# Decay table rows by scaled exponentials, and the last down operand split ahead of the last up sums

## The chip, the cores and the metric

The kernel runs on one core of a Trainium2 chip. Its engines are named as in the profile: PE (matrix products; PEld is its weight load), DVE, ACT, POOL, and SP, which here only issues transfers. The metric is the device time of one execution in microseconds (us), the median of several runs.

## The reference

One block of a network: a state-space convolution and a bilinear gated unit, each behind a layer norm that is scaled and shifted by a conditioning vector. L is 2048, D is 640, N is 192, F is 1536.

```python
mod = (silu(c) @ w_mod).reshape(1, 6, 1, 640)          # sa, ca, ga, sb, cb, gb
h = layernorm(x) * (1 + ca) + sa                       # x is (1, 2048, 640)
# the convolution: one kernel K of length L for each channel d
A = dt * (A_re + 1j * A_im)                            # dt = exp(log_dt), A is (640, 192)
K = einsum("dn,dnl,dn->dl", C, exp(A[:, :, None] * arange(L)), dt * B).real
y = irfft(rfft(pad(K)) * rfft(pad(h.T)))[:, :L].T + h * Dskip
x = x + ga * y
h = layernorm(x) * (1 + cb) + sb
x = x + gb * (((h @ w_gate) * (h @ w_up)) @ w_down)
```

The change lies in exp(A l), whose absolute value is exp(dt A_re l), a decay, and in the last product, with w_down.

## The kernel before

**Tables.** The 640 channels are five blocks `db` of 128, and each block has two halves `hf` of four pieces, so there are 40 pieces `n`. A power exp(A l) is built from a decay and a phase. The positions l are split into high and low parts, so a decay table is an outer product of two short tables: `RH` (eleven rows of 96 numbers a half, for factors 1536, 1024, 512, 0, 8, 16 ... 56 of the logarithm of the decay) and `LP` (positions 64 l) or `LQ` (positions 0 to 7, grown by doubling from the rows of `RL`, whose factors are 1, 2, 4, with amplitudes in its fourth row).

`u_seeds(db)` is a generator that makes these seeds in segments named by letters. Those that matter: `s_d` shifts phases; `s_r(h)` multiplies the logarithms of the decay, which PE has transposed into PSUM (`ps`), by a small constant tile `mults` on DVE, into RL and RH (L521, L523); `s_x` takes a square root and an absolute value; `s_e` takes the exponentials on ACT (seven into LP with the constant scales 64 l, one over all of RH, one over RL, both in place); `s_f` works out the arctangent's argument; `s_g` copies the amplitudes into RL (L571) and takes the arctangent of `pta`; `s_h` transposes it on PE; `s_v` turns it into phases on DVE (L580), from which POOL makes its phase seeds (L584, L585). All of ACT's operations go through one helper and have the line L135. For the first block the halves go apart, the second half's exponentials late; from the second block on a segment does both halves together.

POOL then makes, piece by piece, the phases `Pha`, `Phb` and the decay products `EQ` (from LQ and RH) and `EP` (from LP and RH), all on L649. ACT takes sines and cosines of the phases (`tra`, `trb`), DVE multiplies these with EP and EQ (`k_mul`, L731: `QtA`, `PtAa`, `PtAb`, `QtB`, `PtB`), and PE sums them into the kernel (`kg`, L745 and L760). EP and EQ have two buffers, so POOL's piece n+2 waits until DVE has done the products of piece n. Between these stand the stages of the Fourier transforms (L782 to L942).

**The gated unit.** F is cut in twelve tiles `f`, and the tokens into two halves of two blocks `tb` each. Up and gate products are made with operands that are split into a high and a low part (`hilo`, L992: ACT writes the high part, DVE the difference). For a tile, `y_1`, `z_1`, `y_2`, `z_2`, `y_3` run matmuls (L1028) and sums of them on DVE (L1385, L1397, L1398, L1416, L1405) with the product on DVE (L1410) or POOL. `d_prep(tb, f)` splits a tile of activations and its down weights for the down products (`down`, L1455), and issues a transfer of further weights for odd f; its first two pairs go into `e` and `wsgh`, `wsgl`, the later ones into `sh`, `sl`.

**What sets the order.** Every engine's instructions stand in the order in which the program is written. In the table phase a table of numbers, `SCHED`, gives each step its slot; in the gated unit the order of the calls in the loop does. An engine that waits holds up all that stands behind.

Of the kernel before, what the change touches and what calls it, by code (L numbers as in the profile page):

```python
# [19 lines left out]
P = 128  # L20
D = 640
# [4 lines left out]
NF = F // P  # L26
# [12 lines left out]
    fo=(22003, 31003, 31005, 35001),  # L39
    e0=(-87000,),  # L40
    mc=((31004, 39005, 40006, 43001, 52000), (34000, 53002, 60000, 62000, 69002), (58000, 91004, 92001)),
    q=((22004, 32000, 39001, 40005, 42006, 44000, 44001, 44002, 51000, 51001, 56001, 56002, 57000, 57002), (66002, 89000, 95003, 101000, 107000, 107001, 111000, 112000, 123000, 123003, 124001, 131000, 131003, 131004), (137001, 175000, 176001, 186009, 188001, 189001, 197003, 197004, 201000, 201001, 203002, 204001, 204002, 206001), (210002, 226000, 252005, 264003, 265002, 268001, 268002, 268003, 268005, 272001, 275000, 277000, 280002, 281001)),
    pre=(((56000, 73001, 78000), (40007, 61001, 66003), (76004, 82000, 86001), (88001, 95001, 97002)), ((119002, 127004, 132000), (131002, 131005, 135002), (86005, 99001, 100000), (118000, 118003, 118005)), ((143001, 160000, 160003), (153002, 172001, 172003), (181000, 186005, 186007), (173000, 178000, 178001)), ((221001, 252001, 252006), (224002, 242001, 242004), (245001, 261000, 261001), (281002, 281005, 285000)), ((317000, 335000, 336003), (265003, 298000, 298001), (297000, 315001, 315002), (182002, 196000, 196001))),
    c=(((161005, 162006, 165000, 166001), (122000, 122002, 154000, 155002), (144001, 144002, 167002, 168004), (125000, 125002, 141001, 141002)), ((208003, 217002, 220007, 224000), (201002, 201003, 205000, 211000), (181001, 181002, 198000, 200001), (168003, 170002, 184001, 186003)), ((292002, 295005, 308002, 308006), (245002, 249000, 253002, 253003), (254006, 256002, 278002, 281004), (291000, 291006, 302001, 303000)), ((319002, 321001, 329000, 332001), (337001, 337008, 346000, 349002), (351000, 351001, 360000, 364002), (363002, 365005, 365009, 370000)), ((375000, 379000, 391000, 392004, 393000, 403000), (386001, 386002, 392000, 393001, 394000, 404000), (380002, 385001, 388005, 392001, 392002, 392003), (365006, 371002, 392005, 396000, 398000, 404001))),
    d=(((376000, 388003, 388004), (206000, 206003, 210000), (222000, 225000, 225001), (283001, 284003, 291002)), ((236000, 244002, 248001), (251001, 261002, 262001), (267001, 270000, 270002), (224004, 240000, 244001)), ((340000, 358000, 358001), (354000, 367000, 367002), (319004, 338000, 339005), (309002, 325001, 332000)), ((397001, 401001, 409000), (406000, 414001, 414002), (402000, 414000, 431011), (411000, 424000, 431009)), ((404002, 406001, 407000, 412002), (409002, 412001, 419000, 419001), (425001, 425002, 429000, 431003), (404003, 409001, 415000, 415001))),
# [27 lines left out]
    xs='ababaaaabababa',  # L73
)
SEG0 = ("l", "a", "b", "c", "ud", "r", "x", "e", "f", "G", "g", "D", "h", "v", "R", "")
SEG = ("l", "a", "b", "c", "ud", "D", "r", "R", "x", "E", "f", "g", "h", "v")
P_PH, P_EP, P_MOD = 3, 6, 1


# [50 lines left out]
def tile_kernel(ctx: ExitStack, tc: tile.TileContext, I, out):  # L130
# [3 lines left out]
    def act(o, i, f=AF.Copy, **kw):  # L134
        return S.activation(o, i, f, **kw)  # L135
# [13 lines left out]
    sm = const.tile([P, 16], F32, name="sm")  # L149
    halfpi, dt, dt2 = sm[:, 10:11], sm[:, 0:NB], sm[:, NB : 2 * NB]  # L150
    V.memset(halfpi, math.pi / 2)
    mults = const.tile([P, 14], F32, name="mults")
    for k, m in enumerate((1536, 1024, 512, 0, 8, 16, 24, 32, 40, 48, 56, 1, 2, 4)):
        V.memset(mults[:, k : k + 1], float(m))
    shl = const.tile([P, 11], I32, name="shl")
    for k in range(11):
        V.memset(shl[:, k : k + 1], k + 1)
# [259 lines left out]
    LQ = pk1.tile([P, 96, 8], F32, name="LQ")  # L417
    LP = pk1.tile([P, 3, 96, 8], F32, name="LP")
    LH = pk1.tile([P, 192, 8], I32, name="LH")
    V.memset(LP[:, :, :, 0], 1.0)  # L420
    RH = pk1.tile([P, 3, 11, 96], F32, name="RH")
    RL = pk1.tile([P, 2, 4, 96], F32, name="RL")
    DH = [pk1.tile([P, 4, 192], I32, name=f"DH{i}") for i in range(3)]
    DL = [pk1.tile([P, 4, 192], I32, name=f"DL{i}") for i in range(2)]
# [3 lines left out]
    def u_seeds(db):  # L428
# [10 lines left out]
        dc = dt[:, db : db + 1]  # L439
        hs = (slice(0, 4), slice(4, 8))  # L440
        Dh, Dl = ([R[(2 * db + h) % len(R)] for h in range(2)] for R in (DH, DL))
        Rh, Rl = ([R[:, (2 * db + h) % R.shape[1]] for h in range(2)] for R in (RH, RL))

        def halves(R, hh):

            a, b = ((2 * db + h) % R.shape[1] for h in (hh[0], hh[-1]))
            return R[:, a : a + len(hh)] if a <= b else R[:, 2::-2]
# [3 lines left out]
        T = {}  # L451
# [10 lines left out]
        def free(h, *kinds):  # L462

            hf = 2 * db + h
            for k_ in kinds:
                if k_ in ("ph", "ep", "eq") and hf >= 3:
                    need(1, k_, 4 * (hf - 3) + 3)
                elif k_ in ("lh", "lq") and hf >= 2:
                    need(1, k_, hf - 2)
# [46 lines left out]
            mark("step", 2 * db + h)  # L516

        def s_r(h):
            ps = T["ps"]
            free(h, "ep", "eq", "lq")  # L520
            V.tensor_tensor(g4(Rl[h])[:, 0:3], ps[:, 0, hs[h]].unsqueeze(1).to_broadcast([P, 3, 4, 24]),  # L521
                            mults[:, 11:14].unsqueeze(2).unsqueeze(3).to_broadcast([P, 3, 4, 24]), op=OP.mult)
            V.tensor_tensor(g4(Rh[h]), ps[:, 0, hs[h]].unsqueeze(1).to_broadcast([P, 11, 4, 24]),  # L523
                            mults[:, 0:11].unsqueeze(2).unsqueeze(3).to_broadcast([P, 11, 4, 24]), op=OP.mult)

        def s_u():
            V.tensor_tensor(u, u, T["q"][:, 0], op=OP.add)
# [5 lines left out]
            V.tensor_scalar(pe[:, 1], x, 0.0, 0.5, op0=OP.is_ge, op1=OP.subtract)  # L533

        def s_e(*hh):
            lp, rh, rl = (halves(R, hh) for R in (LP, RH, RL))
            for l in range(1, 8):
                act(lp[:, :, :, l], rl[:, :, 0], AF.Exp, scale=64.0 * l)
            act(rh, rh, AF.Exp)
            act(rl[:, :, 0:3], rl[:, :, 0:3], AF.Exp)  # L540
            for h in hh:
                mark("lp", 2 * db + h)

# [34 lines left out]
        def s_v():  # L578
# [8 lines left out]
            for h in range(2):  # L587
# [1 line left out]
            mark("seeds", db)  # L589

        one = lambda f, *a: lambda: f(*a)
        steps = dict(l=s_l, a=s_a, b=s_b, c=s_c, d=one(s_d, 0), D=one(s_d, 1), r=one(s_r, 0), R=one(s_r, 1), u=s_u, x=s_x,
                     e=one(s_e, 0), E=one(s_e, 0, 1), f=s_f, G=s_G, g=s_g, h=s_h, v=s_v)
        if db == 0:
            LATE.append(lambda: s_e(1))
# [816 lines left out]
    def y_3(i):  # L1412
        ps = pa(side=i % NF == NF - 1)
        prod(ps, [(WT[i], 6 + k, HX[1], k) for k in range(2)] + [(WU[i], 3, HX[1], 2)])
        c = S67.pop(i)
        V.tensor_tensor(c, ps, c, op=OP.add)  # L1416
        G.tensor_tensor(a_tile(NF + i % NF), c, ZT.pop(i), op=OP.mult)
# [107 lines left out]
    for half in range(2):  # L1525
        i0 = half * NF
        if half == 0:

            new_s()
            new_h2()  # L1530
            H = iter(T0["hd"])
            seq = [(sums_u, 0), (x_1, 2), (x_2, 2, False), (x_c, 2), (split_u, 0, "a"), (split_u, 0, "b")]
            seq += [(tokens2, 1, 1, 0, False), (tokens2, 1, 1, 2, True), (s_sums, 0), (tokens2, 1, 1, 1, False), (tokens2, 1, 1, 3, False), (s_sums, 1)]
            seq += [(tokens2, 1, 1, 4, False), (x_1, 3), (x_2, 3, False)]
            seq += [(s_split, k, j) for j in (2, 1) for k in range(2)] + [(s_one, 4), (split_u, 0, "c"), (s_split, 0, 3), (s_split, 1, 3)]
            seq += [(s_one, 2), (s_one, 3), (s_split, 0, 4), (s_split, 1, 4), (s_five,), (x_c, 3), (sums_u, 1), (raw,), (raw_u, 2), (res_l, 0, 1)]
            seq += [(y_1, 0), (split_g, AHEAD), (z_1, 0), (y_2, 0), (split_u, 1), (sums_u, 2), (raw_u, 3), (y_3, 0), (z_2, 0), (fold, 0)]
            for g_, *a_ in seq:
                at((next(H),), once(g_), *a_)
            due(433)  # L1540
            assert not jobs
            PRE[0] = False
        else:
            for j in range(AHEAD):
                if LEAD <= j + 1 < AHEAD:
                    split_g(i0 + j + 1)
                x_1(i0 + j)
                x_2(i0 + j)
# [12 lines left out]
            res_l(3, 1)
        for f in range(1 - half, NF):
            i = i0 + f
            y_1(i)
            if f + AHEAD < NF:
                split_g(i + AHEAD)
            z_1(i)
            late = 0 < f <= NF - AHEAD
            if late:
                x_1(i + AHEAD - 1)  # L1570
            y_2(i)
            if f + 1 < NF:
                split_u(i + 1)
            if f + 2 < NF:
                sums_u(i + 2)
            if f + 3 < NF:
                raw_u(i + 3)
            if late:
                x_2(i + AHEAD - 1)
            y_3(i)  # L1580
            z_2(i)
            if half == 0:
                fold(f)
            if f >= NF - 2:
# [38 lines left out]
```

## Time and profile before

| | |
|---|---|
| median of three runs | 964.85 us (964.2 to 965.12) |
| profiled execution | 960.78 us, of which the span of the trace 959.0 |
| granted PE clock, mean | 0.978 |
| busy PE, DVE, ACT, POOL | 863.3, 757.6, 569.7, 566.6 us |
| HBM traffic | 108.36 MB read, 38.86 MB written |

The span is one execution, from its first to its last record. A row of the timeline has the start, the time from there to the end of the last of its instructions, engine, line, operation, destination and sources, shape and count; a bracket at its end tells how long the engine stood idle before it and which instruction ended that. Rows overlap a little, since an engine starts the next instruction before the last has drained. The tables end near 420 us, the gated unit's products run from about 503 to 951.

### The profile page before, as it was taken

The page shows a single profiled execution, that of the slowest core. Times are in us where ns is not written, and L with a number is a line of the kernel's source. Part 1 is how long each engine was busy: PE and PEld are TensorE (multiplying, and loading weights), DVE is VectorE, ACT ScalarE, POOL GpSimd, SP SyncE. Part 2 cuts the span into 40 slices and gives each one's busy share as a digit, 9 for nine tenths or more (in the row PEclk, how much of TensorE's full clock was granted, in tenths as well). Part 3 has the DMA queues.
Part 4 walks back from the last instruction along what each step waited for, and adds up shares of the span by engine and source line. Part 5 has one row for each costly group of instructions (what it writes and reads, how often), then busy time and mean ns, then how long its engine had stood idle before and what let it go on. Part 6 is the DMA issues. An engine that isn't in the chain of part 4 may idle for free.

```text
span 959.0 us, 26424 instructions
## 1 busy us (share of the span) xinstructions
PE 863.3 (90%) x11070; PEld 715.4 (75%) x11070; DVE 757.6 (79%) x1328; ACT 569.7 (59%) x1022; POOL 566.6 (59%) x419
## 2 busy tenths in 40 slices
PE   2878876898798689889889999999999999999998
PEld 1565655676675467678568888889998888889998
DVE  8998688888889988888899777786677877687452
ACT  6899988887987879754773322225555322223330
POOL 5999999799799999940135866721021544451000
PEclk9977999999999899999999999999999999999999
DMA  8487575434455655478854355155536222212241
GB/s 304 150 289 243 164 222 194 138 112 129 139 183 157 178 148 159 126 228 245 234 157 121 99 192 180 40 192 165 193 137 219 84 83 82 83 55 84 82 166 55
DMA packets 141320, 148.94 MB, mean 155 GB/s; under 512 B 8208, under 2 KB 119568, under 8 KB 139792
## 3 DMA queue, kind: packets, MB, share of 16 engines
q1 hardware_dynamic: 139904, 145.80, 48.4%
q8 instruction: 87, 1.43, 0.6%
q10 hardware_dynamic: 1296, 1.44, 0.5%
q14 instruction: 33, 0.27, 0.1%
HBM read 108.36 MB, written 38.86 MB: 154 GB/s over the span
## 4 chain that ended last, share of the span: by engine, by line
PE 46%; DVE 6%; issue 1%; ACT 1%; POOL 1%; DMA 0%; SPq 0%; DVEq 0%; ACTq 0%
PE pa L1028 26%; PE pa L1455 17%; PE psg L1028 1%; DVE sl L992 1%; DVE wtl L992 0%; PE psg L1108 0%; DMA TVb<-WD 0%; PE psg L1455 0%; DVE a L1147 0%; DVE wsgl L992 0%; ACT hfb L135 0%; PE psg L1162 0%; DVE st L1081 0%; DVE xb L1468 0%; DVE hl L1149 0%
## 5 line engine op out<-in xcount | busy, mean ns | idle before, releaser
L649 POOL TENSOR_TENSOR EQ<-LQ,RH 128x1536 f32<-128x1536 f32 x40 | 124.1, 3103 | 1.1 <-DVE QtB L731 1.1
L135 ACT ACTIVATE z<-pa 128x512 f32<-128x512 f32 x24 | 14.3, 598 | 167.6 <-PE pa L1028 114.7
L992 DVE TENSOR_TENSOR wsgl<-wga,wsgh 128x640 fp32r<-128x640 f32 x72 | 67.6, 943 | 46.5 <-ACT wsgh L135 46.5
L135 ACT ACTIVATE wsgh<-wga 128x640 fp32r<-128x640 f32 x72 | 52.3, 732 | 66.5 <-PE pa L1455 30.2
L1399 POOL TENSOR_TENSOR z<-z,s 128x512 f32<-128x512 f32 x24 | 33.4, 1390 | 88.6 <-DVE s L1398 88.6
L1004 POOL TENSOR_TENSOR tf<-wur,wgb 128x256 f32<-128x256 f32 x24 | 18.8, 782 | 99.6 <-DVE wtl L992 58.9
L649 POOL TENSOR_TENSOR EP<-LP,RH 128x768 f32<-128x768 f32 x40 | 65.7, 1650 | 11.6 <-DVE PtB L731 11.5
L1455 PE MATMUL pa<-wsgh,sh 128*128 128x384 f32 (+1 forms) x295 | 68.6, 311 | 0.0
L1455 PE MATMUL pa<-wsgl,sh 128*128 128x384 f32 (+1 forms) x295 | 68.2, 310 | 0.0
L1455 PE MATMUL pa<-wsgh,sl 128*128 128x384 f32 (+1 forms) x295 | 68.2, 310 | 0.0
L649 POOL TENSOR_TENSOR Pha<-LH,DH 128x1536 int32<-128x1536 int32 (+1 forms) x21 | 62.4, 2971 | 1.3 <-ACT tra L135 1.1
L649 POOL TENSOR_TENSOR Phb<-LH,DH 128x1536 int32<-128x1536 int32 x20 | 62.2, 3112 | 0.0
L992 DVE TENSOR_TENSOR wtl<-tf,wth 128x256 fp32r<-128x256 f32 (+1 forms) x72 | 58.8, 843 | 0.0
L731 DVE TENSOR_TENSOR QtA<-tra,EQ 128x1024 f32<-128x1024 f32 x44 | 51.8, 1214 | 8.0 <-POOL LQ L643 3.2
L1397 DVE TENSOR_TENSOR s<-pa,s 128x512 f32<-128x512 f32 x24 | 16.6, 690 | 42.9 <-PE pa L1028 37.9
L731 DVE TENSOR_TENSOR QtA<-trb,EQ 128x1024 f32<-128x1024 f32 x36 | 42.7, 1215 | 9.6 <-ACT trb L135 3.9
L760 PE MATMUL kg<-QtB,PtB 64*32 64x64 f32 x2560 | 45.3, 220 | 4.3 <-issue 2.2
L760 PEld LDWEIGHTS kg<-QtB,PtB 64*32 64x32 f32 x2560 | 38.4, 108 | 11.8 <-issue 5.9
L1028 PE MATMUL pa<-sh,wtl 128*128 128x512 f32 x144 | 44.6, 391 | 0.9 <-DVE wtl L992 0.9
L1455 PEld LDWEIGHTS pa<-wsgh,sl 128*128 128x128 f32 x295 | 45.3, 188 | 0.0
L1455 PEld LDWEIGHTS pa<-wsgh,sh 128*128 128x128 f32 x295 | 45.3, 188 | 0.0
L1455 PEld LDWEIGHTS pa<-wsgl,sh 128*128 128x128 f32 x295 | 45.3, 188 | 0.0
(653 smaller groups left out, 2854.5 us busy)
## 6 DMA issues: line engine op xcount, KB each, us to landing
wga<-wdg SPq DMA_DIRECT2D x24, 640.0 KB, 4.3
wga<-B_w_gate SPq DMA_DIRECT2D x12, 640.0 KB, 5.9
wgb<-B_w_gate SPq DMA_DIRECT2D x24, 320.0 KB, 3.3
wur<-B_w_up SPq DMA_DIRECT2D x24, 320.0 KB, 4.0
xb<-x2d SPq DMA_DIRECT2D x6, 1280.0 KB, 8.6
t_ti<-w_mod SPq DMA_DIRECT2D x3, 1600.0 KB, 8.6
t_tw<-w_mod SPq DMA_DIRECT2D x3, 1600.0 KB, 9.5
WD<-Wa SPq DMA_DIRECT2D x8, 512.0 KB, 3.7
```

What stands on the lines that cost most here:

```text
L135: return S.activation(o, i, f, **kw)
L649: G.tensor_tensor(o.rearrange("p x (h l) -> p x h l", l=8), lo.unsqueeze(2).to_broadcast([P, rows, nh, 8]), hi.rearrange("p h x -> p x h") ...
L731: V.tensor_tensor(t, tr, e.unsqueeze(1).to_broadcast([P, 2, R, 32]), op=OP.mult)
L760: PE.matmul(kg[j * 32 : j * 32 + 32, dd, :], PtB[lo : lo + 64, c, r, :], QtB[lo : lo + 64, c, r, :], start=False, stop=dd == 7 and c == 1, ...
L992: V.tensor_tensor(lo, v, hi, op=OP.subtract)
L1004: G.tensor_tensor(t[:, 0:2], u[:, 0:2], g[:, 0:2], op=OP.subtract)
L1028: PE.matmul(ps, w[a][:, k], x[b][:, l], start=n == 0 and m == 0, stop=n == 2 and m == len(ks) - 1)
L1397: V.tensor_tensor(S67[i], ps, S6[i], op=OP.add)
L1399: G.tensor_tensor(ZT[i], ZT[i], S67[i], op=OP.add)
L1455: PE.matmul(ACC[tb][t][c], x[:, ts], w[:, cs], start=st, stop=f == NF - 1 and n == 2 and (one or t % 2 == 1))
```

## The change

`mults` and its fourteen memsets go; RH's row for factor 0 is set to 1.0 once. DVE no longer makes products: it copies the logarithms into RL's first row, one copy for both halves (for the first block one each). ACT makes each row of RH and RL with an exponential of its own, which reads that row and has the factor as its constant scale. RL's first row is written last, in place, and waits for the reads ahead of it on the same engine. Waits for free buffers of EP and EQ move from `s_r` to `s_e`. For each block from the second on, two segments become one, and a slot of the table `q` is dropped. In the gated unit `d_prep` of the last tile is called ahead of that tile's `y_3` and `z_2`.

```diff
-    q=((22004, ..., 44000, 44001, 44002, 51000, ...), ...
+    q=((22004, ..., 44000, 44001, 51000, ...), ...
-SEG = ("l", "a", "b", "c", "ud", "D", "r", "R", "x", "E", "f", "g", "h", "v")
+SEG = ("l", "a", "b", "c", "ud", "D", "S", "x", "E", "f", "g", "h", "v")
-    mults = const.tile([P, 14], F32, name="mults")
-    for k, m in enumerate((1536, 1024, 512, 0, 8, 16, 24, 32, 40, 48, 56, 1, 2, 4)):
-        V.memset(mults[:, k : k + 1], float(m))
+    V.memset(RH[:, :, 3], 1.0)
...
         def s_r(h):
-            ps = T["ps"]
-            free(h, "ep", "eq", "lq")
-            V.tensor_tensor(g4(Rl[h])[:, 0:3], ps[:, 0, hs[h]].unsqueeze(1).to_broadcast([P, 3, 4, 24]),
-                            mults[:, 11:14].unsqueeze(2).unsqueeze(3).to_broadcast([P, 3, 4, 24]), op=OP.mult)
-            V.tensor_tensor(g4(Rh[h]), ps[:, 0, hs[h]].unsqueeze(1).to_broadcast([P, 11, 4, 24]),
-                            mults[:, 0:11].unsqueeze(2).unsqueeze(3).to_broadcast([P, 11, 4, 24]), op=OP.mult)
+            for i in h:
+                free(i, "lq")
+            rl = RL[:, 0:2, 0].rearrange("p h (s r) -> p h s r", r=24)[:, h[0] : h[-1] + 1]
+            V.tensor_copy(rl, T["ps"][:, 0, hs[h[0]].start : hs[h[-1]].stop].rearrange("p (h s) r -> p h s r", s=4))
...
         def s_e(*hh):
+            for h in hh:
+                free(h, "ep", "eq")
             lp, rh, rl = (halves(R, hh) for R in (LP, RH, RL))
             for l in range(1, 8):
                 act(lp[:, :, :, l], rl[:, :, 0], AF.Exp, scale=64.0 * l)
-            act(rh, rh, AF.Exp)
-            act(rl[:, :, 0:3], rl[:, :, 0:3], AF.Exp)
+            for k in (2, 1, 0):
+                act(rh[:, :, k], rl[:, :, 0], AF.Exp, scale=512.0 * (3 - k))
+            for k in range(4, 11):
+                act(rh[:, :, k], rl[:, :, 0], AF.Exp, scale=8.0 * (k - 3))
+            for k in (2, 1, 0):
+                act(rl[:, :, k], rl[:, :, 0], AF.Exp, scale=float(2**k))
...
+            if f == NF - 1:
+                d_prep(2 * half, 1)
             y_3(i)
             z_2(i)
             if half == 0:
                 fold(f)
-            if f >= NF - 2:
-                d_prep(2 * half, f - NF + 2)
+            if f == NF - 2:
+                d_prep(2 * half, 0)
```

Line numbers move by two at most. The order on three engines' pieces follows, of before and of after. First DVE at the seeds of block 3 (near 248 us): `psfa` is PSUM, `psfc` the argument for the next step, L868 a Fourier stage.

```order
L731 TENSOR_TENSOR QtA<-tra,EQ_141 128x32x32 x2
L731 TENSOR_TENSOR PtAa<-trb,EP_143 128x1024
L521 TENSOR_TENSOR RL<-psfa,mults 128x288
L523 TENSOR_TENSOR RH<-psfa,mults 128x1056
L521 TENSOR_TENSOR RL<-psfa,mults 128x288
L523 TENSOR_TENSOR RH<-psfa,mults 128x1056
L731 TENSOR_TENSOR PtB<-tra,EP_143 128x512
L731 TENSOR_TENSOR QtB<-tra,EQ_141 128x16x32 x2
L533 TENSOR_SCALAR psfc<-ptb 128x192
```

```order
L733 TENSOR_TENSOR QtA<-tra,EQ_126 128x32x32 x2
L733 TENSOR_TENSOR PtAa<-trb,EP_128 128x1024
L520 COPY RL<-psfa 128x2x96
L733 TENSOR_TENSOR PtB<-tra,EP_128 128x512
L733 TENSOR_TENSOR QtB<-tra,EQ_126 128x16x32 x2
L529 TENSOR_SCALAR psfc<-ptb 128x192
```

Four products stand as one copy now, straight ahead of the same PtB. Second, ACT at the same block (near 255 us), from the table load for the square root to the arctangent of `pta`.

```order
L135 ACT_TABLE_LOAD
L135 ACTIVATE ptb<-ptb 128x192
L135 ACTIVATE psfc<-ptb 128x192
L135 ACT_TABLE_LOAD
L135 ACTIVATE LP<-RL 128x192 x7
L135 ACTIVATE RH<-RH 128x2112
L135 ACTIVATE RL<-RL 128x2x288
L135 ACT_TABLE_LOAD
L135 ACTIVATE trb<-PtAb 128x512
L135 ACTIVATE pta<-pta 128x192
```

```order
L135 ACT_TABLE_LOAD
L135 ACTIVATE ptb<-ptb 128x192
L135 ACTIVATE psfc<-ptb 128x192
L135 ACT_TABLE_LOAD
L135 ACTIVATE LP<-RL 128x192 x7
L135 ACTIVATE RH<-RL 128x2x96 x10
L135 ACTIVATE RL<-RL 128x2x96 x3
L135 ACT_TABLE_LOAD
L135 ACTIVATE trb<-PtAb 128x512
L135 ACTIVATE pta<-pta 128x192
```

Two long instructions are thirteen short ones; nothing else moved on ACT. Third, DVE at the end of the first token half's up products (near 634 us): `psg` is PSUM, `a` an activation tile, `e` and `wsgl` what the down products read.

```order
L1398 TENSOR_TENSOR s_8714<-z,s_8714 128x512
L1416 TENSOR_TENSOR s_8735<-psg,s_8735 128x512
L1405 TENSOR_TENSOR s_8714<-psg,s_8714 128x512
L1410 TENSOR_TENSOR a_8520<-a_8520,s_8714 128x512
L992 TENSOR_TENSOR e<-a_7456,e 128x512
L992 TENSOR_TENSOR wsgl<-wga,wsgh 128x640
L992 TENSOR_TENSOR sl<-a_7457,sh 128x512
```

```order
L1400 TENSOR_TENSOR s_8752<-z,s_8752 128x512
L994 TENSOR_TENSOR e<-a_7494,e 128x512
L994 TENSOR_TENSOR wsgl<-wga,wsgh 128x640
L1418 TENSOR_TENSOR s_8773<-psg,s_8773 128x512
L1407 TENSOR_TENSOR s_8752<-psg,s_8752 128x512
L1412 TENSOR_TENSOR a_8558<-a_8558,s_8752 128x512
L994 TENSOR_TENSOR sl<-a_7495,sh 128x512
```

The two split rows stand three rows earlier, behind the sums that are ready and ahead of those that wait for `psg`. The order on PE and POOL is as before.

More of the change, by code (lines that the diff above doesn't have):

```diff
@@ L41 @@
     mc=((31004, 39005, 40006, 43001, 52000), (34000, 53002, 60000, 62000, 69002), (58000, 91004, 92001)),
-    q=((22004, 32000, 39001, 40005, 42006, 44000, 44001, 44002, 51000, 51001, 56001, 56002, 57000, 57002), (66002, 89000, 95003, 101000, 107000, 107001, 111000, 112000, 123000, 123003, 124001, 131000, 131003, 131004), (137001, 175000, 176001, 186009, 188001, 189001, 197003, 197004, 201000, 201001, 203002, 204001, 204002, 206001), (210002, 226000, 252005, 264003, 265002, 268001, 268002, 268003, 268005, 272001, 275000, 277000, 280002, 281001)),
+    q=((22004, 32000, 39001, 40005, 42006, 44000, 44001, 51000, 51001, 56001, 56002, 57000, 57002), (66002, 89000, 95003, 101000, 107000, 107001, 111000, 123000, 123003, 124001, 131000, 131003, 131004), (137001, 175000, 176001, 186009, 188001, 189001, 197003, 201000, 201001, 203002, 204001, 204002, 206001), (210002, 226000, 252005, 264003, 265002, 268001, 268002, 268005, 272001, 275000, 277000, 280002, 281001)),
     pre=(((56000, 73001, 78000), (40007, 61001, 66003), (76004, 82000, 86001), (88001, 95001, 97002)), ((119002, 127004, 132000), (131002, 131005, 135002), (86005, 99001, 100000), (118000, 118003, 118005)), ((143001, 160000, 160003), (153002, 172001, 172003), (181000, 186005, 186007), (173000, 178000, 178001)), ((221001, 252001, 252006), (224002, 242001, 242004), (245001, 261000, 261001), (281002, 281005, 285000)), ((317000, 335000, 336003), (265003, 298000, 298001), (297000, 315001, 315002), (182002, 196000, 196001))),
@@ L419, in tile_kernel @@
     LH = pk1.tile([P, 192, 8], I32, name="LH")
+    RH = pk1.tile([P, 3, 11, 96], F32, name="RH")
     V.memset(LP[:, :, :, 0], 1.0)
-    RH = pk1.tile([P, 3, 11, 96], F32, name="RH")
+    V.memset(RH[:, :, 3], 1.0)
     RL = pk1.tile([P, 2, 4, 96], F32, name="RL")
@@ L441, in u_seeds @@
         Dh, Dl = ([R[(2 * db + h) % len(R)] for h in range(2)] for R in (DH, DL))
-        Rh, Rl = ([R[:, (2 * db + h) % R.shape[1]] for h in range(2)] for R in (RH, RL))
+        Rl = [RL[:, h] for h in range(2)]
         def halves(R, hh):
@@ L591, in u_seeds @@
         one = lambda f, *a: lambda: f(*a)
-        steps = dict(l=s_l, a=s_a, b=s_b, c=s_c, d=one(s_d, 0), D=one(s_d, 1), r=one(s_r, 0), R=one(s_r, 1), u=s_u, x=s_x,
+        steps = dict(l=s_l, a=s_a, b=s_b, c=s_c, d=one(s_d, 0), D=one(s_d, 1), r=one(s_r, (0,)), R=one(s_r, (1,)), S=one(s_r, (0, 1)), u=s_u, x=s_x,
                      e=one(s_e, 0), E=one(s_e, 0, 1), f=s_f, G=s_G, g=s_g, h=s_h, v=s_v)
```

## The prediction

> **What bounds the kernel now.** I read the page first, then busy time by stretches of 40 us, then the waits of the engine that is full in a stretch, then the rows around the edits. From the page, busy shares and the chain that ended last by line:
>
> ```profile
> PE 863.3 (90%) x11070; PEld 715.4 (75%) x11070; DVE 757.6 (79%) x1328; ACT 569.7 (59%) x1022; POOL 566.6 (59%) x419
> PE pa L1028 26%; PE pa L1455 17%; PE psg L1028 1%; DVE sl L992 1%; DVE wtl L992 0%; PE psg L1108 0%; DMA TVb<-WD 0%; PE psg L1455 0%; DVE a L1147 0%; DVE wsgl L992 0%; ACT hfb L135 0%; PE psg L1162 0%; DVE st L1081 0%; DVE xb L1468 0%; DVE hl L1149 0%
> ```
>
> These averages hide two halves. Stretches, with the busy us of PE, PEld, DVE, ACT and POOL:
>
> ```profile
> 80.00:120.00 40.00, 33.02 (x680) 23.51 (x682) 28.96 (x46) 38.51 (x66) 38.46 (x28) 0.87 0.66 210
> 520.00:560.00 40.00, 40.00 (x179) 33.11 (x178) 32.47 (x47) 10.59 (x24) 29.77 (x27) 1.00 0.49 153
> 600.00:640.00 40.00, 38.92 (x185) 32.54 (x184) 33.38 (x47) 11.42 (x25) 23.82 (x20) 1.00 0.30 104
> ```
>
> While tables are made (here 80 to 120) POOL is full and ACT as full; DVE has a quarter free. In the gated unit PE is full, but for 1.08 us in the last stretch. POOL's waits from 40 to 430 us, the longest three kinds that the edits can reach:
>
> ```profile
> POOL EP L649 <- DVE PtB L731: 11.5, 3, 6.3
> POOL EQ L649 <- DVE QtB L731: 1.1, 1, 1.1
> POOL DL L585 <- DVE ptb L580: 0.6, 1, 0.6
> ```
>
> So only about 13 us of table time are POOL's to lose by waiting, and what DVE saves counts only in them.
>
> **Part 1: products leave DVE.** DVE first, then ACT and POOL, around the seeds of block 3:
>
> ```profile
> 248.54 0.44 DVE L521 TENSOR_TENSOR RL<-psfa,mults 128x288 f32<-128x288 f32 x1
> 251.60 0.68 DVE L731 TENSOR_TENSOR PtB<-tra,EP 128x512 f32<-128x512 f32 x1
> 249.38 0.60 ACT L135 ACTIVATE tra<-ab 128x512 f32<-128x512 f32 x1
> 252.42 1.66 POOL L649 TENSOR_TENSOR EP<-LP,RH 128x768 f32<-128x768 f32 x1 [6.27 <-DVE PtB L731]
> ```
>
> The four products take 251.60-248.54 = 3.06 us a block, 1.53 a half; five blocks make 15.3. A copy of 128x2x96 takes their place, about 0.3 (the L580 row below moves as many elements in 0.36), five make 1.5. DVE loses 13.8 us, nearly all beside POOL's work. Only in block 3 do the products stand straight ahead of the PtB for which POOL waits. PtB needs `tra`, ready at 249.98, so it can start at 250.05: the 6.27 wait shrinks by 1.55. The fourteen memsets and the one new memset of RH's row lie ahead of any input's arrival: 0.
>
> **Part 2: more exponentials on ACT.** ACT in block 3:
>
> ```profile
> 254.71 2.68 ACT L135 ACTIVATE LP<-RL 128x192 f32<-128x192 f32 x7
> 257.18 1.97 ACT L135 ACTIVATE RH<-RH 128x2112 f32<-128x2112 f32 x1
> 259.05 0.67 ACT L135 ACTIVATE RL<-RL 128x576 f32<-128x576 f32 x1
> 259.74 1.28 ACT L135 ACT_TABLE_LOAD   x1
> 261.57 0.35 ACT L135 ACTIVATE pta<-pta 128x192 f32<-128x192 f32 x1
> 261.82 0.58 ACT L135 ACTIVATE ghc<-psfa 128x512 f32<-128x512 f32 x1
> ```
>
> RH and RL cost 259.74-257.18 = 2.56 us; thirteen rows of 128x192 replace them. Their pitch is not in the trace, so bounds: from below the slope between the two long rows, (1.97-0.67)/(2112-576) = 0.85 ns an element, 0.163 a row with no fixed cost, 2.1 in all (-0.4); from above LP's pitch, (257.18-254.71)/7 = 0.353, 4.6 in all (+2.0). I take the arctangent's 261.82-261.57 = 0.25, since it too writes 192 neighbours where LP writes every eighth element: 13 x 0.25 + 0.1 to drain = 3.35, so +0.8 a block; the last row's wait for ACT's own reads is in the upper bound. The Trainium skill ("ScalarE: Activation LUTs", What ACT_TABLE_LOAD costs) gives an activation with immediate scale a fixed 186 ns plus 0.833 ns an element, 93 ns of it overlapped; by that, splitting two instructions into thirteen adds an estimated 1.0 us a block, and the sum below would come out about 0.8 later. The trace's 0.35 duration and 0.25 pitch agree with it.
>
> What waits behind these rows: the table load, the arctangent, its transposes on PE, L580 on DVE, L585 on POOL. The rows: three for block 1, two each for blocks 2, 3 and 4.
>
> ```profile
> 94.03 0.35 ACT L135 ACTIVATE pta<-pta 128x192 f32<-128x192 f32 x1
> 94.86 0.49 PE L458 MATMUL psfa<-ct,pta 128*128 128x128 f32 x2
> 96.16 0.39 POOL L585 TENSOR_TENSOR DL<-ptb 128x96 int32<-128x96 int32 x1 [0.61 <-DVE ptb L580]
> 178.29 0.36 DVE L580 TENSOR_SCALAR ptb<-psfc 128x192 int32<-128x192 f32 x1 [0.87 <-PE psfc L460]
> 178.92 0.39 POOL L585 TENSOR_TENSOR DL<-ptb 128x96 int32<-128x96 int32 x1
> 263.39 0.36 DVE L580 TENSOR_SCALAR ptb<-psfc 128x192 int32<-128x192 f32 x1 [1.37 <-PE psfc L460]
> 264.90 0.39 POOL L585 TENSOR_TENSOR DL<-ptb 128x96 int32<-128x96 int32 x1
> 333.94 3.26 POOL L649 TENSOR_TENSOR EP<-LP,RH 128x768 f32<-128x768 f32 x2 [0.89 <-DVE PtB L731]
> 342.96 0.39 POOL L585 TENSOR_TENSOR DL<-ptb 128x96 int32<-128x96 int32 x1
> ```
>
> - Block 1: the arctangent ended at 94.38, and PE came to it from other matmuls, with no idle time, at 94.86. Of +0.8 some 0.4 is hidden there, +0.45 reaches L585, which already waits.
> - Block 2: L580 waits for PE and ends 0.27 before L585; +0.8 makes L585 late by +0.55.
> - Block 3: POOL arrives 1.55 earlier (part 1), but L580 follows the arctangent's end (261.92) by 1.47 and waits for it through PE; with +0.8 it runs near 264.25 to 264.6, so L585 starts at 264.65: -0.25 and not -1.55. The arctangent is late next.
> - Block 4: PtB's 0.89 wait goes (its products too stand just ahead), but the arctangent, +0.8, puts L585 near 343.35: +0.4.
>
> **Prologue (block 0, halves apart).**
>
> ```profile
> 14.93 0.43 ACT L135 ACTIVATE RL<-RL 128x288 f32<-128x288 f32 x1
> 15.96 3.25 POOL L649 TENSOR_TENSOR EP<-LP,RH 128x768 f32<-128x768 f32 x2
> 18.43 0.39 ACT L135 ACTIVATE RL<-trb 128x96 f32<-128x96 f32 x2 [3.06 <-PE trb L460]
> 20.55 0.79 PE L458 MATMUL trb<-ct,pta 128*128 128x128 f32 x2 [2.17 <-ACT pta L135]
> 22.36 0.38 POOL L585 TENSOR_TENSOR DL<-ptb 128x96 int32<-128x96 int32 x1 [0.66 <-POOL ptb L584]
> 37.47 3.10 POOL L649 TENSOR_TENSOR EQ<-LQ,RH 128x1536 f32<-128x1536 f32 x1 [1.07 <-DVE QtB L731]
> ```
>
> One half's products (1.53, less a copy of 0.17) stand ahead of the work that feeds ACT's 18.43 and PE's 20.55, so L580 comes 1.36 earlier and L585's 0.66 wait ends; the second half's products stand ahead of the QtB for which POOL waits 1.07. Both go: -1.7. Against that, the exponentials of 128x96 ended at 15.36; at the two copies' pitch, 0.39-0.25 = 0.14, thirteen end near 15.9, just before EP's 15.96; at LP's they would delay EP by 0.4. I take -1.4, between 0 and -1.7.
>
> **Part 3: the last down operand.**
>
> ```profile
> 634.08 0.69 DVE L1416 TENSOR_TENSOR s<-psg,s 128x512 f32<-128x512 f32 x1 [1.41 <-POOL z L1399]
> 636.62 0.68 DVE L992 TENSOR_TENSOR e<-a,e 128x512 fp32r<-128x512 f32 x1
> 637.22 0.81 DVE L992 TENSOR_TENSOR wsgl<-wga,wsgh 128x640 fp32r<-128x640 f32 x1
> 637.35 0.56 PE L1455 MATMUL pa<-wsgh,e 128*128 128x384 f32 x2 [0.91 <-DVE e L992]
> 638.09 0.56 PE L1455 MATMUL pa<-wsgl,e 128*128 128x384 f32 x2 [0.17 <-DVE wsgl L992]
> 629.10 0.62 ACT L135 ACTIVATE e<-a 128x512 fp32r<-128x512 f32 x1
> 629.62 0.73 ACT L135 ACTIVATE wsgh<-wga 128x640 fp32r<-128x640 f32 x1
> ```
>
> The two split rows take 637.96-636.62 = 1.34 and their inputs are ready at 630.35; DVE idles 1.41 before 634.08. They fit: PE's 0.91 and 0.17 go, -1.1, and each later split row is 1.34 earlier too, so the next operand is not late. Were the idle gone, L1416 and the sums behind it would start up to 1.34 later, still ahead of PE's need. SP's issue of the next down weights, which stands behind the split, moves earlier with it; nothing waits there. The second half's end has no such gap on PE: 0. Bounds -1.1 and 0.
>
> **Sum.** -1.4 +0.45 +0.55 -0.25 +0.4 -1.1 = -1.35 us. The profiled execution took 960.78 (span 959.0 and 1.78 around it), 4.07 below the median of 964.85; the sum makes it 959.4, and the same step from the median gives 963.5. What can be told from no change is 0.2%, 1.93 us.
>
> **Rivals.**
> - *ACT's extra is hidden, POOL's waits follow DVE.* If the arctangent gets through because DVE, 1 to 3 us earlier, starts ACT's chains sooner, then -1.7 -1.55 -0.89 -1.08 = -5.2: 959.6. For it: ACT's sines take their products from DVE, which come earlier. Against: 38.51 of 40 busy in 80 to 120.
> - *The new rows cost LP's pitch* (slower). At 0.353 a block of ACT is +2.0, L585 is late by 1.6, 1.75, 0.95 and 1.6, the prologue keeps 1.0, part 3 stays: +3.8, 968.6. It passes the 0.2% from a pitch of about 0.31. For it: same line, function and scale form as LP. Against: the stores are neighbours. The Trainium skill ("SBUF — State Buffer", Specifications) has accesses that cross to a new 16-byte line pay a penalty, which would put LP's 0.35 down to its stride; no run here has yet shown the cause.
> - *The prologue's gain is lost* (EP waits for the exponentials, or the QtB is held by ACT): the sum without it is +0.05: 964.9.
>
> **How the numbers follow.** The sum 0.48, hidden extra 0.22, LP's pitch 0.14, lost prologue 0.16. The likeliest, 963.5, has its own range of 962.0 to 965.5 (prologue 0.3 better, exponentials 0.05 a row either way). From 959.9 to 967.2 the range takes in the sum, the lost prologue, over half of the first rival and the better part of a pitch between 0.25 and 0.31: some 0.8. Faster than 962.92: the first rival and 0.4 of the sum's chance, 0.41; slower than 966.78: most of the pitch case, 0.15; between them 0.44.
>
> **What would show it.** In the trace after: the products gone and DVE's busy time down by about 14 us; RH and RL rows at a pitch of 0.25 and the time from the first LP row to the table load longer by 0.8; POOL's waits at 22.36 and 37.47 gone, that at 252.42 near 4.7, and new waits of 0.5 to 1.3 at L585 of blocks 2 to 4; PE without a gap near 637. The last EP of POOL would come 0.2 to 0.3 earlier, and the gated unit end another 1.1 earlier. A pitch over 0.3, waits of POOL for the exponentials themselves, or a clock that differs between the runs would make it wrong.

## The result: 0.56% slower, by more than the tables

The changed kernel takes 968.86 us (median of 14 runs, 965.45 to 974.97) against 964.13 for the kernel before on the same chip (14 runs): a ratio of 1.0056, with a 95% interval of 1.0042 to 1.0071. Forecast were 963.5 and a range that ended at 967.2. The profiled execution took 967.17 us, with a span of 965.3 (before: 960.78 and 959.0).

Busy time of the changed kernel:

```profile
PE 867.6 (90%) x11070; PEld 719.7 (75%) x11070; DVE 746.2 (77%) x1301; ACT 575.9 (60%) x1088; POOL 568.1 (59%) x419
```

DVE lost 11.4 us, where the forecast was 13.8: the rows that split down weights (`wsgl`) took 2.8 us more in all, 70.4 against 67.6. ACT gained 6.2. But PE is busy 4.3 us longer with the same 11070 matmuls, which nothing in the diff asks for.

**The table phase.** ACT in block 3, the rows that answer to 257.18 to 259.74 before:

```profile
257.21 2.64 ACT L135 ACTIVATE RH<-RL 128x192 f32<-128x192 f32 x10
259.75 0.99 ACT L135 ACTIVATE RL<-RL 128x192 f32<-128x192 f32 x3
260.76 1.28 ACT L135 ACT_TABLE_LOAD   x1
```

Thirteen rows take 260.76-257.21 = 3.55 us where two took 2.56: +0.99. POOL's seeds of blocks 0, 1, 3 and 4 after:

```profile
21.97 0.38 POOL L587 TENSOR_TENSOR DL<-ptb 128x96 int32<-128x96 int32 x1
92.73 0.40 POOL L646 TENSOR_TENSOR LQ<-RL 128x96 f32<-128x96 f32 x1 [0.92 <-ACT RL L135]
96.20 0.39 POOL L587 TENSOR_TENSOR DL<-ptb 128x96 int32<-128x96 int32 x1 [1.14 <-DVE ptb L582]
264.93 0.39 POOL L587 TENSOR_TENSOR DL<-ptb 128x96 int32<-128x96 int32 x1
346.88 0.39 POOL L587 TENSOR_TENSOR DL<-ptb 128x96 int32<-128x96 int32 x1 [2.33 <-issue]
```

The prologue's wait is gone, and POOL runs 1.3 us ahead of before until block 1. There it waits for ACT's last exponential (a wait that was not there before) and then for the arctangent, and is at 96.20 where it was at 96.16. Block 3 ends as before too; block 4 is 3.9 us late (342.96 before), and the wait of 2.33, for which the profile names no releaser, ends just behind DVE's L582 (346.39 and 0.36 long). PE's and ACT's rows in block 4, first before, then after, show part of the reason (`prm` holds the amplitudes that PE transposes ahead of the arctangent, `pta`):

```profile
337.47 1.10 PE L760 MATMUL kg<-QtB,PtB 64*32 64x64 f32 x64
337.98 0.58 ACT L135 ACTIVATE ghc<-psfa 128x512 f32<-128x512 f32 x1
339.56 0.37 PE L887 MATMUL psfb<-TVa,t_ti 64*128 64x128 f32 x1
341.54 0.49 PE L458 MATMUL psfa<-ct,pta 128*128 128x128 f32 x2
```

```profile
335.44 1.10 PE L762 MATMUL kg<-QtB,PtB 64*32 64x64 f32 x64
339.72 0.58 ACT L135 ACTIVATE ghc<-psfa 128x512 f32<-128x512 f32 x1
340.35 0.80 PE L456 MATMUL psfa<-ct,prm 128*128 128x128 f32 x2 [3.81 <-ACT ghc L135]
341.49 0.58 PE L889 MATMUL psfb<-TVa,t_ti 64*128 64x128 f32 x1
345.21 0.79 PE L456 MATMUL psfa<-ct,pta 128*128 128x128 f32 x2
```

PE waits 3.81 us for copies out of PSUM into `ghc`, which stand on ACT behind the longer exponentials. They start 1.74 us later than before (339.72-337.98), and PE's last matmuls ahead of the wait 2.03 us earlier (337.47-335.44): the wait opens from both sides. The 32 matmuls of L889 then take 3.72 us (345.21-341.49) and took 1.98. The granted clock says why: it is half (busy time by engine in this stretch, then the clock), before and after:

```profile
340.00:345.00 5.00, 4.51 (x66) 2.78 (x66) 3.83 (x5) 4.99 (x10) 4.62 (x11) 1.00 0.19 71
```

```profile
340.00:345.00 5.00, 4.65 (x38) 4.29 (x38) 2.69 (x4) 3.92 (x7) 2.98 (x6) 0.50 0.00 0
```

The arctangent's transposes stand behind these matmuls, and L585 (now L587) behind them. The half clock is not new, though. Just ahead it stood in the kernel before, and not in the changed one, a likely reason why PE now comes to the copies sooner; from 333 to 337, before and after:

```profile
333.00:337.00 4.00, 3.24 (x28) 2.87 (x30) 3.97 (x7) 3.99 (x9) 3.11 (x3) 0.50 0.39 106
```

```profile
333.00:337.00 4.00, 3.08 (x96) 2.51 (x95) 3.88 (x7) 3.99 (x11) 4.00 (x3) 1.00 0.50 135
```

**The gated unit.** DVE at the end of the first token half:

```profile
637.24 0.68 DVE L994 TENSOR_TENSOR e<-a,e 128x512 fp32r<-128x512 f32 x1
637.84 1.92 DVE L994 TENSOR_TENSOR wsgl<-wga,wsgh 128x640 fp32r<-128x640 f32 x1
639.68 0.68 DVE L1418 TENSOR_TENSOR s<-psg,s 128x512 f32<-128x512 f32 x1
```

The split fits ahead of the sums, which don't wait any more, though its second row takes 1.92 us and not 0.81, and PE's gap there is gone, as forecast. But the unit's pace is lower. ACT's copies `z`, one per up tile, and its `wsgh`, one per down tile, wait for PE where they stand at even distances; there their distance is PE's pace. Before:

```profile
786.35 0.60 ACT L135 ACTIVATE z<-pa 128x512 f32<-128x512 f32 x1 [7.97 <-PE pa L1028]
798.59 0.60 ACT L135 ACTIVATE z<-pa 128x512 f32<-128x512 f32 x1 [7.97 <-PE pa L1028]
887.91 0.74 ACT L135 ACTIVATE wsgh<-wga 128x640 fp32r<-128x640 f32 x1 [2.26 <-PE pa L1455]
891.43 0.74 ACT L135 ACTIVATE wsgh<-wga 128x640 fp32r<-128x640 f32 x1 [2.26 <-PE pa L1455]
```

After:

```profile
790.49 0.60 ACT L135 ACTIVATE z<-pa 128x512 f32<-128x512 f32 x1 [8.06 <-PE pa L1030]
802.83 0.60 ACT L135 ACTIVATE z<-pa 128x512 f32<-128x512 f32 x1 [8.06 <-PE pa L1030]
889.19 0.74 ACT L135 ACTIVATE wsgh<-wga 128x640 fp32r<-128x640 f32 x1 [2.34 <-PE pa L1457]
892.79 0.74 ACT L135 ACTIVATE wsgh<-wga 128x640 fp32r<-128x640 f32 x1 [2.34 <-PE pa L1457]
```

12.24 us an up tile became 12.34, and 3.52 a down tile 3.60, at a granted clock of 1.00 in both and with PE never idle in these stretches. The groups of down matmuls show it as the mean of one (busy us, mean ns), before and after:

```profile
L1455 PE MATMUL pa<-wsgh,sh 128*128 128x384 f32 (+1 forms) x295 | 68.6, 311 | 0.0
```

```profile
L1457 PE MATMUL pa<-wsgh,sh 128*128 128x384 f32 (+1 forms) x295 | 69.6, 314 | 0.0
```

The experiments stand in the order in which they were made; the first eight follow another theory than this pace.

### The profile page after: what moved, and what is told of

Same layout as the page of the kernel before. It is cut to its first block, busy times and chain, and to the rows that moved or that the text cites. A ratio compares the mean times of both kernels' runs of the same rounds, so it can differ in the third digit from the quotient of the medians.

```text
span 965.3 us, 26463 instructions
## 1 busy us (share of the span) xinstructions
PE 867.6 (90%) x11070; PEld 719.7 (75%) x11070; DVE 746.2 (77%) x1301; ACT 575.9 (60%) x1088; POOL 568.1 (59%) x419
## 4 chain that ended last, share of the span: by engine, by line
PE 47%; DVE 5%; ACT 1%; issue 1%; DMA 1%; DVEq 0%; SPq 0%; ACTq 0%
PE pa L1030 28%; PE pa L1457 16%; PE psg L1030 1%; DMA wgb<-B_w_gate 1%; DVE st L1083 1%; DVE sl L994 1%; PE psg L1164 1%; PE psg L1110 0%; PE psg L1457 0%; DVE a L1149 0%; ACT wsgh L135 0%; ACT hh L135 0%; ACT xb L135 0%; DVE xb L1470 0%; DVE wsgl L994 0%
## 5 line engine op out<-in xcount | busy, mean ns | idle before, releaser
L994 DVE TENSOR_TENSOR wsgl<-wga,wsgh 128x640 fp32r<-128x640 f32 x72 | 70.4, 981 | 47.9 <-ACT wsgh L135 47.9
```

The costliest lines, as they stand in the source:

```text
L994: V.tensor_tensor(lo, v, hi, op=OP.subtract)
```

## The experiments

Each ran beside the kernel before (medians of it 963.15 to 963.51 us) in 5 to 12 runs of its own, the fewest for the paddings of 32 and 96 bytes (5 and 8), "exponentials only" and "PE kept busy" (6) and "copies between" (8). Theory A at the start: the loss is block 4's, by the wait and the clock just shown.

**Exponentials only.** The split is put back behind the sums.

```diff
-            if f == NF - 1:
-                d_prep(2 * half, 1)
             y_3(i)
...
-            if f == NF - 2:
-                d_prep(2 * half, 0)
+            if f >= NF - 2:
+                d_prep(2 * half, f - NF + 2)
```

> The exponentials and the copy on DVE as in the changed kernel, the split of the last down operand left where it was before. Theory A (the loss comes from block 4's seeds: ACT's longer row of exponentials holds up two copies out of PSUM for which PE waits 3.8 us, PE's clock falls, and L585 comes 3.9 us late): 1.1 us slower than the changed kernel, near 970, with the wait of 3.8 and the late L585 in the trace and PE's gap of 1.1 back near 640. Theory B (the split ahead of the sums costs the time, in the gated unit): near 964 to 965.

Measured: 970.92 us (ratio 1.0095, 1.0071 to 1.0119), with the wait for ghc of 3.87 us and PE's gap of 0.87 back, at 644.20. The loss is in the table edit (which takes `mults` away), not in the split.

**Split only.** The opposite: the kernel before with the second hunk of the diff alone.

> The kernel before with only the split of the last down operand moved. Theory A: 1.1 us faster than before, near 963.0, PE's gap of 0.91 and 0.17 gone. Theory B (the split costs time later, by transfers issued earlier or slower matmuls): 2 to 4 us slower than before, with later products starting late.

Measured: 962.78 (0.9995, 0.9982 to 1.0009). PE's two waits are gone, and the pace is that of before. The sign fits A, but 1.1 us is too little for the interval to show.

**Copies between.** In block 4, ghc's copies stand between the LP rows and the new rows.

```diff
-        for i, seg in enumerate(SEG0 if db == 0 else SEG):
+        for i, seg in enumerate(SEG0 if db == 0 else SEG if db < 4 else SEG[:8] + ("P", "Q") + SEG[9:]):
...      # P: the LP rows at slot 272001; Q: the RH and RL rows at 274000
```

> The changed kernel with one move: in block 4 the two copies into ghc stand on ACT behind the seven LP rows and ahead of the thirteen new rows. Theory A: PE resumes near 338 and not at 340.4, its clock stays up, L585 of block 4 starts 2.5 to 3.5 us earlier than in the changed kernel, and the time is 965.5 to 966.5. Theory C (block 4's lateness is made up later anyway and the loss sits behind the tables): no change, near 968.9.

Measured: 967.07 (1.0043, 1.0025 to 1.0061); the seeds of block 4 in its trace:

```profile
341.24 0.36 POOL L647 COPY LQ<-RL 128x96 f32<-128x96 f32 x1
345.30 0.39 POOL L589 TENSOR_TENSOR DL<-ptb 128x96 int32<-128x96 int32 x1 [1.51 <-issue]
```

```profile
340.00:345.00 5.00, 4.03 (x38) 3.32 (x34) 2.67 (x5) 4.94 (x12) 3.58 (x6) 0.54 0.00 0
```

L585 came only 1.6 us earlier (346.88-345.30). PE's longest wait is down to 1.68 us, but its clock fell all the same, in the midst of L889. A's gain of 2.5 us or more did not come.

**Block 4 as before.** Products on DVE and two long exponentials for `db == 4`.

> The changed kernel with block 4 alone as before (products on DVE, two long exponentials). Theory A: L585 of block 4 within 0.5 us of before, the time near 965. Theory C: no change, near 968.9. If each block gave its own share (0.8 us of ACT each), about 968.

Measured: 962.82 (0.9995, 0.9979 to 1.0012): six us better than the changed kernel, more than A foresaw. It looked like a proof of A. It was not one: to have the products it had to have the tile `mults` back.

**PE kept busy.** The stage ahead of the ghc copies is issued three times over.

```diff
         ph = stage2(Gt, k0, banks())
+        for _ in range(2 if (db, qd) == (2, 0) else 0):
+            stage2(Gt, k0, ph)
```

> The changed kernel with PE kept busy in the gap of block 4: the stage that writes the sources of the two ghc copies is issued three times over (32 matmuls more, some 3.5 us of PE, same result). Theory A1 (an idle PE of 3.8 us lets its granted clock fall to 0.5, and the sixteen pairs of L889 ahead of the arctangent's transposes then take 3.7 us and not 1.9): the L889 rows run at full clock, L585 of block 4 comes 1.5 to 2.5 us earlier than in the changed kernel, time 966 to 967.5. Theory A4 (the wait for ghc alone, whatever the clock): no gain, 969 or later, since PE can't pass the copies any sooner.

Measured: 971.05 (1.0071, 1.0043 to 1.0099). PE and POOL in block 4:

```profile
343.28 0.49 PE L456 MATMUL psfa<-ct,prm 128*128 128x128 f32 x2 [0.43 <-ACT ghc L135]
343.96 0.37 PE L891 MATMUL psfb<-TVa,t_ti 64*128 64x128 f32 x1
345.96 0.49 PE L456 MATMUL psfa<-ct,pta 128*128 128x128 f32 x2
```

```profile
344.47 0.36 POOL L645 COPY LQ<-RL 128x96 f32<-128x96 f32 x1 [1.43 <-DVE RL L573]
347.25 0.39 POOL L587 TENSOR_TENSOR DL<-ptb 128x96 int32<-128x96 int32 x1 [0.22 <-POOL ptb L586]
```

The half clock is confirmed as the cause of the slow matmuls: without the gap the same matmuls take 2.00 us, and L585 follows LQ by 2.78 us, and not by 4.88 (346.88-342.00). Its worth is not: the time did not fall.

**Block 4 taken apart**, three kernels on the kernel before.

```diff
# ACT only: db 4 has the thirteen exponentials, DVE keeps its products
+            if db == 4:
+                V.memset(Rh[h][:, 3], 1.0)
# DVE only: db 4 has the copy, ACT keeps two long exponentials
+            if db == 4:
+                if h == 1:
+                    V.tensor_copy(rl, ps[:, 0].rearrange("p (h s) r -> p h s r", s=4))
+                return
# both
+OLD = (0, 1, 2, 3)
```

> The kernel before with the thirteen new exponentials in block 4 alone, DVE's products kept there too (two small memsets keep the row for factor 0 at 1). Theory A1 with both parts needed (DVE's saving brings PE's stage forward, ACT's lengthening holds the copies back, and only together they make the gap of 3.8 us): PE's wait near 2 us, 0.5 to 1.5 us slower than before, near 964. Theory A2 (ACT's 0.85 us alone opens the gap, since the clock falls at some threshold): 3 to 5 us slower, 966.5 to 968.

> The kernel before with only DVE's side changed in block 4: the copy in place of the products, the two long exponentials kept (so the rows of that block's tables aren't scaled). Theory A1: PE's stage comes 1.5 to 2 us earlier, the copies stay where they were, PE's gap 1.5 to 2 us, no slower than before, 962 to 964. Theory A3 (DVE's saving alone lets PE go idle and its clock fall): 3 us or more slower than before.

> The kernel before with all of the table change in block 4 alone, and no other edit. Theory A1: the whole loss of the change, 5 to 7 us slower than before, near 969, with the gap of 3.8 us and half the clock behind it. If it takes the shifts of the other blocks too (the clock's state on arrival), 0 to 3 us.

Measured: 964.15 (1.0012, 0.9994 to 1.003), 964.01 (1.0006, 0.999 to 1.0023), 965.45 (1.0017, 0.9999 to 1.0035). No part of block 4, nor all of it, costs the 5 to 7 us of A. All of it comes to 1.6 us, with an interval that begins at nothing. Theory A falls as the main cause.

In their traces PE's wait does not come as A1 expected, which saw near 2 us of it from ACT's side. With ACT's longer row alone PE does not wait there, and the 32 matmuls take 1.98 us (343.16-341.18); but its clock is 0.50 from 333 to 341, so PE is late itself. With DVE's copy alone the clock is 1.00 from 336 to 342, PE waits 2.50 and the matmuls take 3.54 (346.31-342.77), and the kernel is no slower for it; with both 1.77 and 3.62 (343.45-339.83). The row of DVE alone:

```profile
342.06 0.49 PE L458 MATMUL psfa<-ct,prm 128*128 128x128 f32 x2 [2.50 <-ACT ghc L135]
```

**The addresses.** What did the slow kernels share? The pace: 3.60 and 12.34 in the changed kernel, in "exponentials only", "copies between" and "PE kept busy"; 3.52 and 12.24 in the other six profiles, whatever their tables. The first four have no tile `mults`. Its 56 bytes a partition, rounded to 64, stood ahead of all later tiles. In the two builds' allocations `wsgh` lies at byte 45536 of a partition before and at 45472 after, `sh`, of another pool, at 135136 in both. Four kernels with no instruction added or changed (the shift issues the fourteen memsets later, still in the prologue), first the decisive two:

```diff
# padding (64 bytes; also 32 and 96), on the changed kernel
+    const.tile([P, 16], F32, name="pad")
     shl = const.tile([P, 11], I32, name="shl")
# shift, on the kernel before
-    mults = const.tile([P, 14], F32, name="mults")
+    mults = pk1.tile([P, 14], F32, name="mults")   # behind all other tables
```

> The changed kernel with an unused tile of 64 bytes a partition where the tile of factors stood, so that every tile allocated behind it lies at its address of before; no instruction differs. Theory P (removing that tile moved the gated unit's weight and activation tiles by 64 bytes against the operands of the other pool, and PE's pace fell: 3.60 us a down tile and 12.34 an up tile in the changed kernel and in its three variants without the tile, 3.52 and 12.24 in the six kernels that have it): 3.52 and 12.24, 3.5 to 4.5 us faster than the changed kernel, near 965. Theory Q (the pace comes from something else that these kernels share, such as the number of ACT's instructions): 3.60 and 12.34, 969.

> The kernel before, with the tile of factors allocated in the table pool and not among the constants, so that all tiles of the gated unit's own pool lie 64 bytes lower, as in the changed kernel; no instruction differs. Theory P: a pace of 3.60 and 12.34 and 3.5 to 4.5 us slower than before, near 967.5. Theory Q: 3.52, 12.24 and no change.

Measured: padding 965.02 (1.0016, 0.9999 to 1.0033), shift 967.26 (1.0047, 1.0025 to 1.0069). The changed kernel with padding:

```profile
521.54 0.60 ACT L135 ACTIVATE z<-pa 128x512 f32<-128x512 f32 x1 [9.38 <-POOL a L1420]
888.84 0.74 ACT L135 ACTIVATE wsgh<-wga 128x640 fp32r<-128x640 f32 x1 [2.26 <-PE pa L1458]
892.36 0.74 ACT L135 ACTIVATE wsgh<-wga 128x640 fp32r<-128x640 f32 x1 [2.26 <-PE pa L1458]
L1458 PE MATMUL pa<-wsgh,sh 128*128 128x384 f32 (+1 forms) x295 | 68.6, 311 | 0.0
```

The kernel before with the shift:

```profile
524.02 0.60 ACT L135 ACTIVATE z<-pa 128x512 f32<-128x512 f32 x1 [9.39 <-POOL a L1417]
784.32 0.60 ACT L135 ACTIVATE z<-pa 128x512 f32<-128x512 f32 x1 [7.62 <-PE pa L1028]
796.66 0.60 ACT L135 ACTIVATE z<-pa 128x512 f32<-128x512 f32 x1 [8.06 <-PE pa L1028]
L1455 PE MATMUL pa<-wsgh,sh 128*128 128x384 f32 (+1 forms) x295 | 69.6, 314 | 0.0
```

Both ways round the pace follows the address: 3.52 and 12.24 with padding, 12.34 and 314 ns with the shift. In time that is 0.40% by the padding (1.0056-1.0016, 3.9 us) and 0.47% by the shift (4.5 us). The traces show that it lies in the unit. From its second copy `z` to the end of the span the changed kernel takes 445.9 us (965.3-519.42) and with padding 441.9 (963.4-521.54); the kernel before takes 443.5 (959.0-515.52) and with the shift 447.5 (971.5-524.02): 4.0 us both ways. Theory P holds, Q falls. The rows of the other two kernels:

```profile
515.52 0.60 ACT L135 ACTIVATE z<-pa 128x512 f32<-128x512 f32 x1 [9.37 <-POOL a L1417]
519.42 0.60 ACT L135 ACTIVATE z<-pa 128x512 f32<-128x512 f32 x1 [9.38 <-POOL a L1419]
```

> The changed kernel with 32 bytes of padding. If any offset against the other pool costs, 3.60 or slower; if the pace follows lines of 64 bytes, another value than at 64; the time follows the pace at about 45 down tiles times the difference.

> The changed kernel with 96 bytes of padding, 32 above the addresses of before. If only the kernels' offset of before is good, 3.60 or slower; if an offset upward is as good or better, 3.52 or less, and a faster version would be had by padding alone.

Measured: 968.9 (five runs; 1.0034, 1.0001 to 1.0067) with a pace of 3.52 and 12.35; 965.01 (1.0014, 0.9991 to 1.0038) with 3.50 and 12.35. So a shift need not cost on both kinds of tile: of the four offsets (-64, -32, 0 and +32 bytes) only -64 slows the down tiles, and only 0 is fast on the up tiles.

**The rest, with the addresses of before.** Copies between, plus padding; and block 0 alone in the new form with the split moved (`OLD = (1, 2, 3, 4)`).

> The changed kernel with the addresses of before (64 bytes of padding) and with the two ghc copies of block 4 ahead of the thirteen new rows. If the two causes add (addresses 3.9, block 4's copies about 1.8 as measured with the addresses shifted), 962.9 to 963.5, within 0.5 us of before; if block 4's lateness costs nothing once the pace is right, 965 as with padding alone.

> Block 0 alone with the new exponentials and the copies, blocks 1 to 4 with products and two long exponentials, the split moved; the tile of factors is kept, so the addresses are those of before. If the prologue's gain of 1.3 us, seen in the trace of the changed kernel up to 91 us, is only lost there because block 1's arctangent comes later, 961.5 to 962; if block 1 absorbs it whatever its exponentials (the copies and the arctangent there wait for work that doesn't move), 962.5 to 963, as with the split alone.

Measured: 966.03 (1.0025, 1.0007 to 1.0043), so moving the copies shows no gain over padding alone (1.0016), against my expectation; and 960.27 (0.9967, 0.9946 to 0.9987), faster than both kernels. The prologue's gain is kept when block 1 keeps its short row of exponentials.

## Why the prediction was wrong

By the ratios, each step being the difference of two kernels and uncertain by 0.2% (2 us) or a little more (the steps add up to the whole by the way they are formed):

| step | kernels | measured | forecast |
|---|---|---|---|
| split | split only - before | -0.5 | -1.1 |
| prologue | block 0 new - split only | -2.7 | -1.4 |
| blocks 1 to 3 | block 4 as before - block 0 new | +2.7 | +0.75 |
| block 4 | padding - block 4 as before | +2.0 | +0.4 |
| addresses | changed - padding | +3.9 | 0 |
| sum | | +5.4 | -1.35 |

One caution for all that follows from single traces. "Split only" has the tables of before, and yet its L585 of blocks 1 to 4 stand at 99.50, 182.95, 269.13 and 347.82: 3.3 to 4.9 us later than before, and in block 4 later than in the changed kernel. A shift of that size in one trace is no proof. The distance from block 3's L585 to block 4's scatters less: 78.06 before, 78.69 in "split only" and 78.91 with the shift, all with the old tables, against 81.95 in the changed kernel, 82.66 in "exponentials only" and 81.79 with padding; but 84.65 and 79.72 with 32 and 96 bytes of padding.

- **The step that failed most is one that the sum does not have.** "The fourteen memsets and the one new memset ... : 0" priced the instructions of `mults` and not its place. Removing it moved the gated unit's own tiles by 64 bytes against the operands of the other pool, and 3.9 of the 5.4 us are that (4.0 in the traces): shown both ways, by padding the changed kernel and shifting the kernel before. No rival covered it.
- **The pitch of the new rows was right.** It was 0.254 us ((259.75-257.21)/10), against 0.25 taken; a block took +0.99 against +0.8, the rest lying in the three in-place rows and the last row's end, though no run took these apart. The estimate from the Trainium skill ("ScalarE: Activation LUTs", What ACT_TABLE_LOAD costs), 1.0, came nearer by luck: it counts eleven more instructions at 93 ns, but not that the thirteen rows hold 192 elements fewer than the two (2496 against 2688), which by the section's 0.833 ns an element makes the estimate 0.86. The slower rival's pitch of 0.353 did not come about.
- **Block 1** was put at +0.45 on top of a kept -1.4. POOL came 1.55 us earlier to LQ and found ACT's exponentials unfinished (0.92), then the arctangent (1.14). The sum let ACT's block move with POOL; ACT's rows there stood within 0.5 us of before, so the block took all the prologue had won: in the trace 1.35. That the prologue's gain lasts without this is shown by block 0 alone in the new form, and by its time, not by this trace.
- **Block 2** came out at +0.26 from block 1's L585 to its own ((179.22-96.20)-(178.92-96.16)), against +0.55; "split only", with the old tables, differs there from before by more (182.95-99.50 = 83.45, and 82.76 before).
- **Block 3** came out at +0.03 against -0.25, near the forecast by luck. POOL's wait for PtB is shorter by 1.91 (4.36 against 6.27) and EP starts 1.55 earlier (250.87), as forecast. But this was not lost to the arctangent: L585 does not wait. It was lost at LQ, which waits for DVE's copy of the amplitudes (L573, at 261.62; L571 at 261.59 before), a chain that the edit did not move and the sum does not have:

```profile
262.30 0.36 POOL L645 COPY LQ<-RL 128x96 f32<-128x96 f32 x1 [2.04 <-DVE RL L573]
```

- **Block 4** was put at +0.4, through the arctangent. The prediction followed what stands behind the arctangent, and not PE, which waits for the two `ghc` copies behind the exponentials on ACT. That this wait brings the half clock is shown by the trace and by the kernel that fills the gap. What opens it is not parted: the copies come 1.74 us later, and PE, at the full clock just ahead, 2.03 sooner; with ACT's row alone PE had the half clock there and did not wait, with DVE's copy alone it had the full clock and waited 2.50. In time block 4 is about 2 us, no larger than the uncertainty of that difference, not the 3.9 of that one trace, and neither filling the gap nor moving the copies got them back. What else they are is open.
- **The split** did in the trace what was forecast (0.91 and 0.17 gone, the next operands no later); in time it is too small to tell from nothing. The traces of the unit tell it: from the second `z` to the end "split only" takes 441.9 us (962.9-521.02) against 443.5 before, and the changed kernel 445.9 against 447.5 (969.1-521.62) in "exponentials only", 1.6 us in both pairs. The two waits are 1.08 of it; where the other 0.5 lies is not shown.

The nearest rival by its number was the slower one, 968.6, but for another reason.

## What to carry to other kernels

When an edit removes or adds a tile, compare the addresses of all that is allocated behind it, and put padding in its place before the edit is judged; a stage that the edit does not touch must keep its pace (us per tile) in the trace, and that is the first thing to look at. An experiment that restores an instruction restores its tiles too: the kernel with block 4 as before seemed to prove a cause that it did not test. Of a longer block on an engine, follow every instruction queued behind it, the small copies above all, and ask which engines come to them sooner or later than before. Before a shift in one trace is called an effect, see how far the same row moves between two kernels that do not differ there.

## What the runs showed that was not expected

- The pace of fp32 matmuls depended on where their operands lie: with no other change, 64 bytes lower made a down matmul 314 ns and not 311, a down tile 3.60 us and not 3.52 (2.3%), an up tile 12.34 and not 12.24 (0.8%). Of the down groups, those with one operand in each pool slowed (`wsgh,sh`), while `wsgh,e`, with both in the moved pool, did not: 310 ns before and with the shift, 308 in the changed kernel and with padding. But of the up groups `sh,wtl`, whose operands both lie in the pool that stayed, slowed too, 391 ns before and 393 with the shift; so the distance between a matmul's own two operands is not the whole rule. Which bits of the address matter was not settled by four offsets.
- PE's clock fell to 0.50 behind an idle time of 3.81 us. The Trainium skill ("TensorE: Matmul & The Clock Gate", Part 1) has it fall to half after an idle window of about 3.4 us. The fall to half agrees; the length does not come out of these traces. In the changed kernel the clock stands at 0.99 from 339.20 to 339.30 and at 0.50 from 339.30 to 339.40, some 2.8 us after PE's last matmul ahead of the wait (336.54). It fell too where no wait just ahead was over 1.68 us (0.54 in copies between), and after a wait of 1.68 in "split only" it stayed at 1.00. What decides is open.
